# Reordering the projections of a segment-recurrent attention kernel: keys and queries first, a different set of refetched weights, longer scratch runs, small loads on another ring

## Chip, cores, metric

One core of one Trainium2 chip. The metric is device time in microseconds (us) of one execution; lower is better. Kernels that are compared ran on the same chip in alternating rounds.

## The reference, cut to what matters

```python
# A: attention over 64 segments of 32 tokens, with 8 memory rows carried from one to the next
mem = mem0                                             # [1, 8, 1024]
for s in range(64):
    h = concatenate([mem, x[:, 32*s : 32*s + 32]])      # 40 rows of 1024
    q, k, v = h @ Wq, h @ Wk, h @ Wv                    # each 1024 -> 32 heads x 128
    p = softmax(mask(q @ k.T * 128**-0.5))
    o = (p @ v) @ Wo                                    # 32 x 128 -> 1024
    mem = o[:, :8];  outs.append(o[:, 8:])
# B: a gated feed-forward (1024 -> 3584 -> 1024) over the 2048 tokens
return g * a + (1 - g) * b                              # g = sigmoid of a row sum
```

All data are bf16. The four projection matrices are 8 MB each. Cut into pieces of 512 KB that makes 64 pieces, and SBUF has room for 52 of them. So 12 places ("slots") are shared by two pieces, one of each half of the heads, and in every segment 12 pieces are fetched anew.

## The kernel before: the parts concerned

The heads are worked in two halves, `r` = 0 and 1; `ua` and `ub` are the halves that come first and second in this segment (they swap from segment to segment, so what the second half used is still there when the next segment starts). `PAIRS` names the pieces that share a slot. `walk` is the order in which PE (TensorE) goes through the 64 pieces. When a piece has been used and its slot is wanted by another, the fetch of that other is issued at once on SP; SP's weight fetches land in the order of their issue (in all 63 segments of the trace before).

```python
PAIRS = {"k": (0, 2), "q": (0,), "v": (0, 1, 2, 3, 4, 6), "o": (0, 2, 4)}    # 12 shared slots
def seq(m, r):
    ...                                            # p: the paired pieces, f: the others
    return p + f if r == 0 else f + p              # paired ones first in half 0, last in half 1
walk = both(0) + one("v", 0) + both(1) + one("o", 0) + one("v", 1) + one("o", 1)   # both: k, q alternating

def spent(k):                                      # after the piece k has been used
    n = home[k]
    done[n] += 1
    if done[n] < len(uses[n]) and uses[n][done[n]] != k:
        fetch(n)                                   # op("sp", dma_start 512 KB)
```

The hooks of a segment, `on(matrix, half, n, what)` = ahead of the n-th piece of that part. Fills (`f1`, `f2`) are projections of the rows that do not depend on the recurrence, computed some segments early; a fill has eight pieces of PE work.

```python
on("v", 0, 0, lambda: evac(bank_of["k", 0], tok));   on("v", 0, 0, lambda: evac(bank_of["q", 0], tok2))
on("v", 0, 4, lambda: trans(kT, tok));               on("v", 0, 7, lambda: trans(qT, tok2))
on("k", 1, 0, lambda: evac(bank_of["v", 0], vA))     # beside the 16 pieces of the second k and q
on("k", 1, 2, lambda: scores(0))
...
on("o", 0, 0, some(f1, 4)); on("o", 0, 0, lambda: trans(kT, tok)); on("o", 0, 0, some(f1, 2))
on("o", 0, 0, lambda: trans_pe(tok2)); on("o", 0, 0, lambda: attend(ua)); on("o", 0, 0, lambda: attend_tail(ua))
on("o", 0, 0, lambda: trans(qT, None)); on("o", 0, 0, some(f1))
on("o", 0, 1, lambda: scores(1, ...))                # behind the first o piece
on("o", 1, 0, lambda: evac(bank_of["v", 1], vA)); on("o", 1, 0, some(f2, 6))
on("o", 1, 0, lambda: attend(ub)); on("o", 1, 0, lambda: attend_tail(ub)); on("o", 1, 0, some(f2))
```

## Time and profile before

| | before |
|---|---|
| median of 3 runs | 2205.21 us (2203.95 to 2216.17) |
| profiled span, granted TensorE clock | 2213.4 us, 0.988 |
| recurrence | 64 segments, 24.25 us each |
| fetches in a segment | 12 of 512 KB on SP (3 k and q, 6 v, 3 o) |

The strips, the instruction lines and the windows that carry the reading are in the prediction below. Here are two more views. First the page's queues and its chain (the work that ended last, followed back):

```profile
q1 hardware_dynamic: 171760, 466.69, 59.2%
q0 software_dynamic: 30432, 56.99, 8.0%
...
PE 60%; DMA 23%; POOL 6%; DVE 6%; issue 3%; ACT 1%; SPq 0%; DVEq 0%; POOLq 0%
```

q1 is SP's ring with the weights, q0 is POOL's. The chain runs through PE for three fifths of the time and through transfers for a quarter. Then PE's list of waits (who waited for whom: us in total, times, longest us):

```profile
PE pb L690 <- DVE kT L680: 42.6, 29, 12.2
PE pb L796 <- issue: 22.0, 18, 1.9
PE pb L711 <- DVE qT L680: 17.8, 59, 0.3
PE pb L796 <- DMA sl<-in_A_Wk_dram: 13.7, 18, 1.5
PE pb L1025 <- ACT a_bf L677: 13.0, 34, 0.4
```

### The profile page before, as it was taken

The page shows a single profiled execution, that of the slowest core. Times are in us where ns is not written, and L with a number is a line of the kernel's source. Part 1 is how long each engine was busy: PE and PEld are TensorE (multiplying, and loading weights), DVE is VectorE, ACT ScalarE, POOL GpSimd, SP SyncE. Part 2 cuts the span into 40 slices and gives each one's busy share as a digit, 9 for nine tenths or more (in the row PEclk, how much of TensorE's full clock was granted, in tenths as well). Part 3 has the DMA queues.
Part 4 walks back from the last instruction along what each step waited for, and adds up shares of the span by engine and source line. Part 5 has one row for each costly group of instructions (what it writes and reads, how often), then busy time and mean ns, then how long its engine had stood idle before and what let it go on. Part 6 is the DMA issues. An engine that isn't in the chain of part 4 may idle for free.

```text
span 2213.4 us, 76738 instructions
## 1 busy us (share of the span) xinstructions
PE 2034.4 (92%) x37840; PEld 934.4 (42%) x32178; DVE 931.1 (42%) x2154; ACT 606.9 (27%) x1296; POOL 625.2 (28%) x1155
## 2 busy tenths in 40 slices
PE   7789998999999999999989999999888999999999
PEld 4334444444444444444444444444344424343343
DVE  6433343334334434434433344344344516254362
ACT  4322222223222232323322232222222303122130
POOL 7223333432433343243334324333321000000000
PEclk9989999999999999999999999999999999999999
DMA  9978887788888888878887888888789400001000
GB/s 366 389 254 277 297 298 271 270 295 303 281 277 314 297 277 304 310 270 299 304 277 271 287 301 289 275 306 297 274 297 371 150 22 29 30 25 34 20 29 20
DMA packets 202660, 528.84 MB, mean 239 GB/s; under 512 B 29592, under 2 KB 46616, under 8 KB 202336
## 3 DMA queue, kind: packets, MB, share of 16 engines
q1 hardware_dynamic: 171760, 466.69, 59.2%
q0 software_dynamic: 30432, 56.99, 8.0%
q8 instruction: 274, 4.49, 0.8%
q10 hardware_dynamic: 144, 0.26, 0.1%
q14 instruction: 50, 0.41, 0.1%
HBM read 490.16 MB, written 33.55 MB: 237 GB/s over the span
## 4 chain that ended last, share of the span: by engine, by line
PE 60%; DMA 23%; POOL 6%; DVE 6%; issue 3%; ACT 1%; SPq 0%; DVEq 0%; POOLq 0%
PE pb L462 16%; PE pb L796 11%; PE pb L779 8%; PE pb L807 7%; DMA a_scr<-a_bf 7%; DMA sl<-in_A_Wk_dram 6%; PE pb L822 5%; DMA sl<-in_A_Wv_dram 4%; PE pb L1135 4%; PE pb L690 3%; DMA sl<-in_A_Wo_dram 3%; POOL v_scr L863 2%; DVE oT L680 2%; DMA xr_scr<-xr 2%; PE pb L837 1%
## 5 line engine op out<-in xcount | busy, mean ns | idle before, releaser
L796 PE MATMUL pb<-sl,hT 128*32 128x512 bf16 x8192 | 665.0, 381 | 48.6 <-issue 22.0
L779 PE MATMUL pb<-sl,hT 128*32 128x512 bf16 x4096 | 398.0, 379 | 0.0
L796 PEld LDWEIGHTS pb<-sl,hT 128*32 128x32 bf16 x8192 | 210.5, 96 | 429.7 <-issue 274.5
L807 PE MATMUL pb<-sl,oT 128*32 128x256 bf16 x8192 | 282.4, 281 | 19.2 <-issue 11.6
L773 POOL COPY oRc<-oT 128x128 bf16<-128x128 bf16 x128 | 96.1, 750 | 654.3 <-DVE oT L680 648.6
L677 ACT ACTIVATE tok<-pb 128x512 bf16<-128x512 f32 x318 | 176.3, 596 | 346.1 <-PE pb L796 320.6
L807 PEld LDWEIGHTS pb<-sl,oT 128*32 128x32 bf16 x8192 | 206.2, 99 | 83.8 <-ACT oT L677 45.2
L822 PE MATMUL pb<-sl,hR 128*32 128x512 bf16 x3072 | 209.9, 384 | 0.0
L462 PE MATMUL pb<-xT,wg 128*128 128x512 bf16 x768 | 182.8, 381 | 5.0 <-DMA wg<-in_B_w_gate_dram 5.0
L680 DVE COPY kT<-pb 128x512 bf16<-128x512 bf16 x128 | 53.2, 416 | 319.0 <-PE pb L690 287.4
L462 PE MATMUL pb<-xT,wu 128*128 128x512 bf16 x768 | 181.8, 380 | 0.0
L680 DVE CAST oT<-pb 128x256 bf16<-128x256 f32 x256 | 96.7, 419 | 182.9 <-PE pb L762 182.9
L690 PE MATMUL pb<-ident,tok 128*128 128x128 bf16 x1272 | 126.6, 222 | 48.9 <-DVE kT L680 42.6
L1135 PE MATMUL pb<-wd,GT 128*32 128x512 bf16 x1568 | 152.2, 379 | 0.0
L779 PE MATMUL pb<-wd,GT 128*32 128x512 bf16 x1568 | 152.2, 379 | 0.0
L677 ACT ACTIVATE vA<-pb 128x512 bf16<-128x512 f32 x128 | 76.4, 597 | 270.5 <-PE pb L796 270.5
L450 ACT ACTIVATE s<-pb 128x512 f32<-128x512 f32 x112 | 66.9, 597 | 291.5 <-PE pb L462 291.5
L690 PEld LDWEIGHTS pb<-ident,tok 128*128 128x128 bf16 x1272 | 72.0, 98 | 158.8 <-DVE kT L680 90.8
L677 ACT ACTIVATE oT<-pb 128x256 bf16<-128x256 f32 x256 | 84.3, 381 | 189.9 <-PE pb L762 189.9
L451 DVE SCALAR_TENSOR_TENSOR tp<-s,pb 128x512 f32<-128x512 f32 x112 | 76.7, 685 | 125.9 <-ACT s L450 125.5
L726 ACT ACTIVATE E<-pb 128x320 bf16<-128x320 f32 x128 | 56.0, 438 | 220.5 <-DVE pb L725 220.5
L462 PEld LDWEIGHTS pb<-xT,wg 128*128 128x128 bf16 x768 | 75.0, 98 | 97.5 <-issue 8.7
(104 smaller groups left out, 2230.3 us busy)
## 6 DMA issues: line engine op xcount, KB each, us to landing
sl<-in_A_Wv_dram SPq DMA_DIRECT2D x394, 512.0 KB, 9.3
sl<-in_A_Wo_dram SPq DMA_DIRECT2D x205, 512.0 KB, 5.9
sl<-in_A_Wk_dram SPq DMA_DIRECT2D x142, 512.0 KB, 7.3
sl<-in_A_Wq_dram SPq DMA_DIRECT2D x79, 512.0 KB, 6.6
qkr<-qk_scr POOLq DMA_DIRECT2D x126, 64.0 KB, 2.2
qk_scr<-stg POOLq DMA_DIRECT2D x59, 128.0 KB, 6.2
wd<-in_B_w_down_dram SPq DMA_DIRECT2D x7, 1024.0 KB, 14.8
xq_scr<-xTp SPq DMA_DIRECT2D x4, 1024.0 KB, 17.3
```

The lines of the kernel that those rows point to most:

```text
L450: op("act", lambda e: e.activation(s1[:, :], hg, ACTF.Square, scale=SQ), rd=[BK(bg)], wr=[s1.r()])
L451: op("dve", lambda e: e.scalar_tensor_tensor(out=t[:, :], in0=s1[:, :], scalar=1.0, in1=hg, op0=ALU.add, op1=ALU.mult), rd=[BK(bg), s1.r() ...
L462: ins = e.matmul(PB[bk][:, 0:FB], lhsT=w[:, kc, cc:cc + 128], rhs=x[:, :, :, kc, :].rearrange("p t i c -> p (t i) c"), start=(kc == 0), st ...
L677: op("act", lambda e: e.activation(o, i, ACTF.Copy), rd=rd, wr=wr)
L680: op("dve", lambda e: e.tensor_copy(o, i), rd=rd, wr=wr)
L690: ins = e.transpose(to, t[:, j * 128:(j + 1) * 128], ident[:, :])
L773: op("pool", lambda e: e.tensor_copy(oRc[:, u, :, :].rearrange("p c (g j) -> p g j c", g=4), diag), rd=[oT.r()], wr=[oRc.r(128 * u, 128 * ...
L779: return e.add_instruction(mybir.InstMatmult(name=nc.get_next_instruction_name(), start_tensor_calc=start, stop_tensor_calc=stop, tile_siz ...
L796: ins = again(e, g, *at, one, end) if k[0] == "q" else e.matmul(*at, start=one, stop=end)
L807: ins = e.matmul(PB[XO][32 * g:32 * g + 32, 0:256], lhsT=oT[:, gp_, 2 * jj + hh, 0:32], rhs=w[:, c:c + 256], start=(r == 0 and one and hh ...
L822: ins = e.matmul(PB[b][32 * g:32 * g + 32, :], lhsT=h[:, k[2], :], rhs=w[:, g * 512:(g + 1) * 512], start=(n == 0), stop=(n == 7))
L1135: ins = again(e, q, *a, j == 0, j == NJ - 1) if hf else e.matmul(*a, start=(j == 0), stop=(j == NJ - 1))
```

## The change

Intent: with k and q of both halves ahead of most v pieces, softmax of the first half lies beside v work; alternating o and v pieces give the second softmax cover; fills stand where PE waited; copies that ACT did alone are shared by ACT and DVE; scratch rows are stored in longer runs by fewer transfers; small loads leave POOL for SP. The layout of the tiles is shuffled so that vA and qT get other bytes, and one v pair becomes an o pair. The core of the diff (the first and last parts and all of the first segment's special cases are cut):

```diff
-        v_scr = nc.dram_tensor("v_scr", [NSEG, NB, 16, 2, 128], BF16)
+        v_scr = nc.dram_tensor("v_scr", [NSEG, NB, 2, 16, 128], BF16)
...
-        vA = al("vA", [128, 4, 128], at=oT.off)
+        vA = al("vA", [128, 4, 128], at=tok.off)
+        qT = al("qT", [128, 4, 4, 32], at=stage.off)
...
-        PAIRS = {"k": (0, 2), "q": (0,), "v": (0, 1, 2, 3, 4, 6), "o": (0, 2, 4)}
+        PAIRS = {"k": (0, 2), "q": (0,), "v": (0, 1, 2, 3, 4), "o": (0, 1, 2, 3)}
...
-        walk = both(0) + one("v", 0) + both(1) + one("o", 0) + one("v", 1) + one("o", 1)
+        V0 = 3
+        walk = both(0) + one("v", 0)[:V0] + both(1) + one("v", 0)[V0:] + [x for y in zip(one("o", 0), one("v", 1)) for x in y] + one("o", 1)
...
-            op("pool", lambda e: e.dma_start(t[:, :, :].rearrange("p k c -> p (k c)"), xq_scr[s // 4, :, s % 4, :]),
+            op(eng, lambda e: e.dma_start(t[:, :, :].rearrange("p k c -> p (k c)"), xq_scr[s // 4, :, s % 4, :]),   # eng="sp"
...                                            # the same for the loads of qkr and vB; one store of v for four, one of q and k for two
+        def trans8(ka, qa, head=False):        # k and q transposed in one group, two halves of one bank
+            def f(e):
+                trans4(e, ka)
+                return trans4(e, qa, head, 512)
...
+            def turn():
+                heads(kT, "act", 0)
+                heads(qT, "dve", 512)
+            on("k", 1, 1, lambda: trans8(tok, tok2));  on("k", 1, 1, turn)
+            on("k", 1, 3, lambda: scores(ua));         on("k", 1, 3, softmax)
+            on("v", 0, V0, lambda: evac(bank_of["k", 1], tok))
+            on("v", 0, V0, lambda: evac(bank_of["q", 1], tok2))
+            def halves(bank):
+                evac(bank, vA, "act", 0, 256)
+                evac(bank, vA, "dve", 256, 512)
+            on("o", 0, 0, some(fa, 1));  on("o", 0, 0, lambda: trans8(tok, tok2))
+            on("o", 0, 0, lambda: halves(bank_of["v", 0]));  on("o", 0, 0, turn)
+            on("o", 0, 0, some(fa, 2));  on("o", 0, 0, lambda: attend(ua, 0))
+            on("o", 0, 0, lambda: attend_tail(ua, 0))
+            on("o", 0, 0, some(fa, 1));  on("o", 0, 0, lambda: scores(ub));  on("o", 0, 0, softmax)
+            on("o", 0, 0, some(fa, 2))
+            if uw is not None:
+                on("o", 0, 0, lambda: load_oR(Q, uw))
+            on("o", 1, 0, lambda: halves(bank_of["v", 1]));  on("o", 1, 0, some(fa))
+            on("o", 1, 0, lambda: attend(ub, 1));  on("o", 1, 0, lambda: attend_tail(ub, 1))
...
+            on("o", 1, 0, some(fb, 4))
```

## The prediction

> **What bounds the kernel now.** The page of the profiled execution first (2213.4 us; the quoted median is 2205.21), its strips of busy tenths:
>
> ```profile
> PE   7789998999999999999989999999888999999999
> PEld 4334444444444444444444444444344424343343
> ...
> DMA  9978887788888888878887888888789400001000
> ```
>
> Slices 3 to 30 are the recurrence over 64 segments, the rest a dense feed-forward part that the diff leaves alone. In the recurrence both PE and the DMA engines are near full, neither quite. The copies that carry the recurrent rows into the next hT run from 144.5 to 1648.1 us, 63 pairs: (1648.1 - 144.5) / 62 = 24.25 us a segment. Everything depends on that number.
>
> Next the instructions of PE in order of time (start, length, and in brackets the idle time before and who ended it):
>
> ```profile
> 614.18 0.40 PE L690 MATMUL pb<-ident,tok 128*128 128x128 bf16 x4
> ...
> 619.19 0.40 PE L796 MATMUL pb<-sl,hT 128*32 128x512 bf16 x4 [0.96 <-DMA sl<-in_A_Wk_dram]
> ...
> 623.41 0.32 PE L711 MATMUL pb<-mS,ident 128*32 128x320 bf16 x4 [0.30 <-DVE qT L680]
> ```
>
> ```profile
> 651.66 1.47 PE L796 MATMUL pb<-sl,hT 128*32 128x512 bf16 x22 [1.47 <-issue]
> ...
> 657.53 0.40 PE L1025 MATMUL pb<-ident,a_bf 128*128 128x128 bf16 x2 [0.39 <-ACT a_bf L677]
> ...
> 670.73 0.40 PE L690 MATMUL pb<-ident,tok 128*128 128x128 bf16 x4 [0.89 <-DVE kT L680]
> ```
>
> The waits are short, of many kinds, and no kind dominates. Summed between 225 and 1584 us they are 112 us, 2.0 us a segment. Then the same stretch by the DMA engines (columns: window, length, busy of PE, PEld, DVE, ACT, POOL, granted clock, DMA share, GB/s):
>
> ```profile
> 610.60:611.60 1.00, 1.00 (x24) 0.32 (x12) 0.00 (x0) 0.00 (x0) 0.94 (x3) 1.00 0.72 233
> ...
> 613.60:614.60 1.00, 1.00 (x20) 0.43 (x16) 0.35 (x1) 0.00 (x0) 0.00 (x0) 1.00 0.94 202
> ...
> 620.60:621.60 1.00, 1.00 (x18) 0.43 (x15) 0.42 (x1) 0.13 (x1) 0.00 (x0) 1.00 1.07 434
> ...
> 631.60:632.60 1.00, 0.61 (x23) 0.50 (x24) 0.00 (x0) 0.00 (x0) 0.98 (x2) 1.00 0.00 0
> ```
>
> This is one period of the weight stream: 12 fetches of 512 KB that are not resident (two k, one q, six v, three o). For some five us from the segment's start the engines are busy and move 130 to 250 GB/s, then 400 to 430, then for about 3 us nothing, because the next fetch is freed only by the next segment's first piece. At 410 GB/s a fetch is 1.28 us, twelve are 15.4. The landings in the trace (mean of the segments with fills, from the hT copy) say the same: first k 5.4, q 7.7, second k 9.4 to 10.4, then one about every 1.3, last v 18.2, last o 21.8 to 23.1. From the last landing to the end of the segment there are 1.2 to 2.4 us. So PE's chain and the weight stream are tied. Segments 60 and 62, which have no fills and so some 3 us less of PE work, still take 23.2 us.
>
> The stores that fall into the slow stretch, from POOL's order of time, are the third piece:
>
> ```profile
> 659.09 0.55 POOL L1009 DMA_DIRECT2D o_scr<-oRc  x1
> 659.62 2.20 POOL L863 DMA_DIRECT2D v_scr<-stg  x4
> 661.82 0.71 POOL L1035 DMA_DIRECT2D a_scr<-a_bf  x1
> ```
>
> and, from the list of waits,
>
> ```profile
> DVE pA L732 <- DMA a_scr<-a_bf: 34.0, 27, 3.1
> ```
>
> POOL issues six to ten transfers one after another around each boundary, 0.55 us each, and the store of a_bf comes last although pA (same bytes) waits for it.
>
> **What the Trainium skill says.** "DMA: Bandwidth & Descriptors", section "Why small descriptors are slow (HBM only)", gives each packet a fixed overhead, 27% for 256 bytes; its table "Specifications" asks for 512 B or more. The change turns 256 B runs of the k/q and v stores into 512 B and 1 KB. The trace agrees in sign only: weight packets of 4 KB took about 160 ns at mid-segment and about 250 ns in the slow stretch; it does not say which store did it. The same page, section "Issuing engines are not separate DMA queues", says that a transfer moved from POOL to SP saves only issue time: here 0.55 us of POOL for some 0.4 us of SP. "Perfetto Trace Analysis", section "Identifying the Most-Contended Engine", warns that matmul busy time overstates how near PE is to its limit; agreed, as the four concurrent matmuls of a piece are each shown as 379 ns while a piece starts every 0.216.
>
> **The change part by part, per segment.** First PE. From the listing, 16 k/q pieces take 3.46 us (0.216 each), seven o pieces 1.53 (0.22). Work that stays: 48 x 0.216 = 10.4; 16 x 0.22 = 3.5; fills, 12 pieces on average x 0.216 = 2.6; Wo fills 4 x 0.21 = 0.8. Sum 17.3. Scores 2 x 0.31, attend with tail and its bubbles 2 x 0.45, the end of the segment (last product, copy, transpose, copy) 0.5: 2.0.
> - Transposes: four groups and on average one of a fill, each 0.42 (0.10 of drain before, three starts of 0.056, 0.15 after): 2.1 now. Merged into groups of eight (0.10 + 7 x 0.056 + 0.15 = 0.64), two and on average half a one: 1.6. Saves 0.5.
> - Waits, 2.0 in idle time and 0.85 as bubbles that count as busy (24.25 - 17.3 - 2.0 - 2.1 = 2.85). The softmax of the first half now begins before the rest of v and is 3.8 us long (616.1 to 619.9) against some 4.5 us of PE work up to its use, so the kT wait of 0.9 goes. qT gets its own bytes: the 0.30 goes. The second softmax lies beside 16 alternating o and v pieces (3.5 us) and fills. The a_bf wait (0.39) is covered by four fill pieces (0.86). New small waits, worked from the copy times of the groups table (ACT 128x512 0.60, DVE 0.42, halves 0.38 and 0.42): tok2 before the second group of eight 0.15; vA before attend 0.2 in each half; kT by ACT behind half of vA 0.1 in each half. Sum 0.75.
> - PE after: 17.3 + 2.0 + 1.6 + 0.75 = 21.7.
>
> Then the stream. Still 12 fetches, one v less and one o more (2 KB packets at 84 ns against 4 KB at 159, so 0.07 us more). Five small loads leave POOL and are issued on SP about 3 us earlier; v stores are one issue instead of four, q and k share one; the a_bf store is among the first. I choose that this takes 1.3 us out of the slow stretch; the trace cannot give it. Second k then lands at 8.1 to 9.1 and is needed at 8.3 to 9 (piece 34 of 64 plus scores and transposes, five v pieces earlier than now): a wait of 0.3 on average. v0 to v2 follow, v3 and v4 by 14.8; the o fetches are freed at 13.3 to 14.6 and land at 16.9 to 21.0. After the last o piece come now 0.86 us of fill and 0.5 of end: 21.0 + 0.2 + 1.4 = 22.6.
>
> Stream 22.6, PE 21.7 + 0.3 for the second k = 22.0. I take 22.5, since the stream's end binds in most segments. Saving 24.25 - 22.5 = 1.75 a segment, 63 segments: 110 us. Prologue and feed-forward unchanged to within a few us. 2205 - 110 = 2095.
>
> **The rivals.**
> - The stream decides alone and longer runs do nothing. Then the last o lands at 22.3, the fills after it add 0.86 with the DMA engines idle, the segment stays at 24: within 2%, 2185 to 2200. For it: segments without fills barely faster. Against: in two segments of four the last landing lies 2.4 us before the end, so PE's own waits bind there.
> - The second k becomes the wait: its window shrinks by about a microsecond, from 8.3 to 7.3 (some 36 pieces to 31), and 0.96 is already lost at 619. If the slow stretch stays, 1.5 to 2 us go back there and the gain is 0.5 a segment, 2170.
> - The stream's slow stretch vanishes almost wholly (it costs 2.6 to 3.6 us against 1.28 a fetch). Then PE binds at 21.5: 2205 - 173 = 2032.
> - SP's ring is in order: a small load whose data or buffer is late holds back the weight fetches behind it. Against: all three are freed before the segment's end, data written segments ago. If it happens, 0.5 us a segment, 30 us lost.
>
> **Range and chances.** The low end is the third rival with some waits left, 2035; the high end lies between the first two, 2165. Above 2161 the change is within 2%: the first rival or a strong second one, together 0.12; slower by 2% needs a stall that I don't see, 0.03; faster 0.85.
>
> **What would show it.** Period of the hT copies 22 to 23; the waits for kT, qT and a_bf gone; PE's idle time near 1 us a segment; DMA share above 0.88 with fewer windows below 250 GB/s near the boundary; the a_bf store landing before pA asks for it; waits left on Wk or Wo. Wrong if Wk waits exceed 1 us a segment, if the slow stretch is as long as now, or if the period stays above 23.5.

## More of the kernel before

Every operation is recorded through one helper, which works out the waits from what is read and written. For PSUM it goes by the bank: engines that touch one bank wait for one another.

```python
if kind == "P":                                    # a PSUM bank
    b = self.banks.setdefault(reg[1], {})
    deps.extend(o for eng, o in b.items() if eng != op.eng)
    b[op.eng] = op
```

## The result, and the profile after

The changed kernel takes **2371.12 us** (median of 4, 2364.87 to 2380.57), the kernel before in the same rounds 2209.35 us: ratio 1.073, 95% interval 1.068 to 1.079. It is slower by 7%. A ratio is the mean time of one kernel's fast runs over that of the other's of the same rounds, so it is not quite the ratio of the medians quoted. The profiled span is 2373.7 us at a clock of 0.958.

The page of the changed kernel (strips as before; PEclk is the granted clock in tenths):

```profile
PE   7778888888888888888888888888787999999999
...
PEclk9989999989999999999999999999988999999999
...
DMA  9967777777877877778878887777878910001000
...
q1 hardware_dynamic: 216240, 483.68, 59.8%
q0 software_dynamic: 22400, 40.56, 5.2%
...
PE 58%; DMA 34%; DVE 3%; ACT 2%; issue 1%; POOL 1%; SPq 1%; POOLq 0%; DVEq 0%; ACTq 0%
```

In the recurrence PE is at 8 where it had been at 9, and the DMA engines, which should have become fuller, went from 8 to 7. Both are less busy: this suggests that something is now in series that was in parallel. The chain names transfers for 34% in place of 23%, and the o weights alone for 16% in place of 3%. PE's list of waits:

```profile
PE pb L812 <- DMA sl<-in_A_Wo_dram: 100.4, 105, 3.6
PE pb L755 <- DVE vA L680: 62.1, 126, 1.0
PE pb L850 <- DMA oR<-o_scr: 42.2, 23, 3.2
PE pb L801 <- DVE hT L680: 18.2, 59, 0.3
PE pb L801 <- DMA sl<-in_A_Wk_dram: 11.5, 19, 1.8
```

PE's waits for kT and a_bf are gone, as intended, and so is DVE's wait for pA (34.0 us before, none after); qT's fell to 10.6 us. In their place stand o weights, vA, and the rows of o for the fills. One segment shows all of it. PE, in order of time (start, length, idle before it and its releaser in brackets):

```profile
702.91 0.30 PE L755 MATMUL pb<-tA,vA 32*128 32x64 bf16 x16 [0.39 <-DVE vA L680]
...
705.43 0.39 PE L812 MATMUL pb<-sl,oT 128*32 128x256 bf16 x8
...
710.02 0.29 PE L755 MATMUL pb<-tA,vA 32*128 32x64 bf16 x16 [0.52 <-DVE vA L680]
...
711.25 1.69 PE L812 MATMUL pb<-sl,oT 128*32 128x256 bf16 x48
714.06 0.40 PE L812 MATMUL pb<-sl,oT 128*32 128x256 bf16 x8 [1.12 <-DMA sl<-in_A_Wo_dram]
715.34 0.40 PE L812 MATMUL pb<-sl,oT 128*32 128x256 bf16 x8 [0.87 <-DMA sl<-in_A_Wo_dram]
```

The first o piece of the segment, at 705.43, frees the first o slot. Its successor and three others are needed from 712 on, and the last two come 1.12 and 0.87 us late. The second vA of this segment, ACT first and then DVE:

```profile
709.13 0.38 ACT L677 ACTIVATE vA<-pb 128x256 bf16<-128x256 f32 x1 [3.58 <-PE pb L801]
```

```profile
709.54 0.42 DVE L680 CAST vA<-pb 128x256 bf16<-128x256 f32 x1 [1.72 <-ACT vA L677]
```

DVE had been idle for 1.72 us and starts 0.03 us after ACT's half has ended: the two halves come out of one bank, and they run one after the other. They take 0.83 us together; the single ACT copy of the kernel before takes 0.597 and lay beside other work. Last, the weight stream and the clock in the same segment (columns as in the prediction's windows):

```profile
703.00:704.00 1.00, 1.00 (x52) 0.74 (x51) 0.96 (x3) 0.62 (x2) 0.00 (x0) 1.00 1.02 389
...
705.00:706.00 1.00, 0.80 (x24) 0.57 (x28) 0.50 (x2) 0.44 (x1) 0.95 (x2) 1.00 0.49 176
706.00:707.00 1.00, 1.00 (x40) 0.77 (x32) 0.90 (x4) 0.00 (x0) 0.00 (x0) 1.00 0.62 139
707.00:708.00 1.00, 1.00 (x36) 0.70 (x28) 0.79 (x3) 0.00 (x0) 0.00 (x0) 1.00 0.80 119
708.00:709.00 1.00, 1.00 (x32) 0.74 (x28) 0.00 (x0) 0.00 (x0) 0.00 (x0) 1.00 0.97 373
...
717.00:718.00 1.00, 0.73 (x8) 0.28 (x8) 0.19 (x1) 0.47 (x2) 0.94 (x3) 0.50 0.00 0
```

For three microseconds in the middle of the segment the stream falls to 119 to 176 GB/s: the v fetches are running out when the first o fetch is issued at 705.87, and that fetch's first packet starts only at 707.05. On average over the segments the DMA engines are busy 0.63, 0.69 and 0.83 of the three microseconds from 14 us after the first k issue; in the kernel before it was 1.00, 0.89 and 0.96. And after the late o pieces the clock is at 0.50, from 716.2 to 719.6 us. In the whole run the records show the clock at half for 202 us, before for 55. The Trainium skill describes such a fall in "TensorE: Matmul & The Clock Gate", section "HAM oscillation — how this bites in real kernels": a wait for data that crosses a window of some 3.4 us lets PE fall back to half rate, and the loss is half of the time at that rate. The trace agrees in the length (31 of the 44 stretches last 3.41 us, 10 more twice that), but not in the waits: here they were 1.12 and 0.87 us. As to the loss, from 717.27 to 718.95 PE's k and q pieces start every 0.42 us, and every 0.22 in the same segment at full clock.

The landings say it most clearly. From the trace, mean of 50 segments, us from the issue of the segment's first k fetch:

```
                         k     q     k   | v ...                                     | o ...
before   landed        4.66  7.02  8.96 | 10.74 12.26 13.57 14.86 16.15 17.47      | 18.85 20.40 21.83
         o issued                                                                    13.70 14.74 15.16
after    landed        4.89  7.10  8.50 | 10.64 12.00 13.47 14.97 16.27            | 18.60 20.64 22.32 23.91
         o issued                                                                    14.27 14.71 15.50 16.20
```

Once several fetches are queued, one lands every 1.3 to 1.6 us. Before, the ring (SP's queue of fetches) holds v fetches until 17.5 us and the o fetches, issued 2.3 to 3.8 us ahead of that, follow at 1.4 to 1.6 us. After, the first o is issued only 2.0 us ahead of the last v's landing at 16.27; it needs 4.3 us from issue to landing and comes 2.33 us behind the last v, and the next comes 2.04 behind it. The last o lands 2.1 us later than before, and the segment is longer by 2.4.

### The profile page after: what moved, and what is told of

Its sections match the earlier page's. It is cut to its first block, busy times and chain, and to the rows that moved or that the text cites. A ratio compares the mean times of both kernels' runs of the same rounds, so it can differ in the third digit from the quotient of the medians.

```text
span 2373.7 us, 77419 instructions
## 1 busy us (share of the span) xinstructions
PE 2059.2 (87%) x38220; PEld 970.0 (41%) x32556; DVE 1007.0 (42%) x2249; ACT 607.0 (26%) x1330; POOL 429.6 (18%) x776
## 4 chain that ended last, share of the span: by engine, by line
PE 58%; DMA 34%; DVE 3%; ACT 2%; issue 1%; POOL 1%; SPq 1%; POOLq 0%; DVEq 0%; ACTq 0%
DMA sl<-in_A_Wo_dram 16%; PE pb L463 15%; PE pb L801 13%; PE pb L784 9%; DMA sl<-in_A_Wk_dram 8%; PE pb L812 5%; PE pb L831 4%; DMA oR<-o_scr 4%; PE pb L1160 4%; DMA sl<-in_A_Wv_dram 3%; PE pb L691 3%; PE pb L850 2%; PE pb L1138 1%; DVE vA L680 1%; ACT vA L677 1%
## 5 line engine op out<-in xcount | busy, mean ns | idle before, releaser
L801 PE MATMUL pb<-sl,hT 128*32 128x512 bf16 x8192 | 742.2, 389 | 34.3 <-DVE hT L680 18.2
L812 PE MATMUL pb<-sl,oT 128*32 128x256 bf16 x8192 | 368.0, 286 | 107.1 <-DMA sl<-in_A_Wo_dram 100.4
L784 PE MATMUL pb<-sl,hT 128*32 128x512 bf16 x4096 | 415.0, 395 | 0.0
L801 PEld LDWEIGHTS pb<-sl,hT 128*32 128x32 bf16 x8192 | 225.3, 98 | 369.3 <-issue 217.8
L831 PE MATMUL pb<-sl,hR 128*32 128x512 bf16 x3072 | 248.4, 403 | 21.9 <-DMA sl<-in_A_Wv_dram 10.7
L677 ACT ACTIVATE tok<-pb 128x512 bf16<-128x512 f32 x253 | 144.1, 596 | 221.6 <-PE pb L801 216.8
L680 DVE CAST a_bf<-pb 128x128 bf16<-128x128 f32 x64 | 18.7, 292 | 342.8 <-ACT a_bf L677 342.8
L680 DVE CAST tok<-pb 128x512 bf16<-128x512 f32 x93 | 64.0, 689 | 170.8 <-PE pb L784 170.8
L850 PE MATMUL pb<-sl,oR 128*32 128x256 bf16 x2016 | 78.4, 304 | 44.4 <-DMA oR<-o_scr 42.2
L463 PEld LDWEIGHTS pb<-xT,wu 128*128 128x128 bf16 x768 | 75.1, 98 | 90.9 <-DMA wu<-in_B_w_up_dram 0.4
L455 DVE SCALAR_TENSOR_TENSOR tp<-tp,pb 128x512 f32<-128x512 f32 x112 | 77.0, 687 | 77.9 <-ACT tp L454 77.9
## 6 DMA issues: line engine op xcount, KB each, us to landing
wd<-in_B_w_down_dram SPq DMA_DIRECT2D x7, 1024.0 KB, 14.9
```

Of the source, the lines that this page charges most:

```text
L455: op("dve", lambda e: e.scalar_tensor_tensor(out=t[:, :], in0=t[:, :], scalar=1.0, in1=hu, op0=ALU.add, op1=ALU.mult), rd=[BK(bu), t.r()], ...
L463: ins = e.matmul(PB[bk][:, 0:FB], lhsT=w[:, kc, cc:cc + 128], rhs=x[:, :, :, kc, :].rearrange("p t i c -> p (t i) c"), start=(kc == 0), st ...
L677: op("act", lambda e: e.activation(o, i, ACTF.Copy), rd=rd, wr=wr)
L680: op("dve", lambda e: e.tensor_copy(o, i), rd=rd, wr=wr)
L784: return e.add_instruction(mybir.InstMatmult(name=nc.get_next_instruction_name(), start_tensor_calc=start, stop_tensor_calc=stop, tile_siz ...
L801: ins = again(e, g, *at, one, end) if k[0] == "q" else e.matmul(*at, start=one, stop=end)
```

## The experiments

In the table, a period of the recurrence and PE's idle time in it are split by who ended the wait (us a segment, 61 segments, matmul records of the trace). "PE" is the period less its idle time, and includes the loss by the half clock.

| kernel | median us | ratio to before | period | PE | idle | Wo | Wk, Wq, Wv | vA | oR | other | half clock | last o lands |
|---|---|---|---|---|---|---|---|---|---|---|---|---|
| before | 2209 | 1 | 24.27 | 22.18 | 2.08 | 0.04 | 0.32 | 0.05 | 0 | 1.67 | 0.45 | 21.83 |
| after | 2371 | 1.073 | 26.66 | 22.52 | 4.13 | 1.58 | 0.30 | 0.95 | 0.64 | 0.66 | 2.63 | 23.91 |
| e4_no_o | 2148 | 0.973 | 23.19 | 21.14 | 2.05 | 0 | 0.51 | 0.95 | 0 | 0.59 | 0.06 | none |
| f2_bno_o | 2192 | 0.992 | 23.94 | 22.07 | 1.88 | 0 | 0.24 | 0.05 | 0 | 1.59 | 0.34 | none |
| f1_bpairs | 2293 | 1.037 | 25.42 | 22.79 | 2.63 | 1.32 | 0.07 | 0.05 | 0 | 1.19 | 1.45 | 23.65 |
| e8_v6p | 2282 | 1.032 | 25.46 | 21.87 | 3.59 | 0.60 | 0.71 | 0.96 | 0.14 | 1.18 | 0.90 | 22.97 |
| g5_order | 2239 | 1.014 | 24.62 | 21.91 | 2.71 | 0.15 | 1.49 | 0.08 | 0 | 0.99 | 0.34 | 22.01 |

The first theory was: PE's own chain did get shorter, as the prediction had it, and what is lost is lost to the o fetches. The rival: the new order of PE is slower in itself, by the copies that were not parallel.

### e4_no_o and f2_bno_o: the o weights are never fetched anew

Wrong: a shared o slot keeps the piece of one half for both (the result still passes within its tolerance).

```diff
-            if done[n] < len(uses[n]) and uses[n][done[n]] != k:
+            if done[n] < len(uses[n]) and uses[n][done[n]] != k and k[0] != "o":
```

e4 is the changed kernel with this line, f2 the kernel before with it.

> The changed kernel, but the o weights are never fetched again once they lie in their slots (wrong result on purpose): 8 fetches a segment instead of 12, everything else the same. Theory W (the o fetches are freed too late and the last one's landing sets the segment's end): PE's waits for Wo (some 180 us over PE and its weight loads) go to nothing, the period falls from 26.6 to about 23.5, time near 2180, ratio 0.99. Rival S (the small loads on SP's ring, the vA and oR waits and the lower granted clock carry the loss): at most 86 us of idle time go, time 2285 or more, ratio above 1.03.

> The kernel before, with the o weights never fetched again (wrong on purpose), the twin of e4_no_o. It shows what PE's own chain costs before the change. If the weight stream was nearly the bound before (as the prediction has it, tied), the time falls a little: period 23 to 23.5, 2130 to 2160, ratio 0.97. If the stream was not on the path before, ratio 0.99 to 1. If the new order is a better chain on PE, as intended, e4_no_o (0.9725) is below this one.

Measured: 2148.47 us (ratio 0.973, 0.969 to 0.976) and 2191.94 (0.992, 0.990 to 0.994). Without o fetches the changed order is faster than the order before by 43 us. So the o stream costs the changed kernel 2371 - 2148 = 223 us and cost the kernel before 18. That settles the first question: PE's chain is better, the stream takes it all back and more. Per segment after and e4 differ by 3.47 us. The table accounts for 3.3 of them: Wo 1.58, oR 0.64, and half of (2.63 - 0.06) of half clock, 1.29 (an estimate), together 3.5, less the 0.2 by which the other weight waits are shorter in after. What stays in e4 is the 0.95 for vA.

```profile
PE pb L755 <- DVE vA L680: 62.5, 127, 1.0
PE pb L801 <- DMA sl<-in_A_Wk_dram: 25.8, 37, 2.3
PE pb L801 <- DVE hT L680: 18.5, 59, 0.3
```

(PE's waits in e4.) f2 missed its first forecast (2130 to 2160): by the fork written ahead of it, the o fetches were not on the path before. Without them a segment takes 23.94 us, with them 24.27, and PE's wait for Wo was 0.04. So PE's chain, with the k and v fetches that it needs, bound, and the stream's end lay behind it without setting the time; f1, next, shows how little room there was.

### f1_bpairs and e1_pairs: the shared pieces alone, both ways

f1 puts a fourth o pair in the place of the sixth v pair in the kernel before, e1 takes it back in the changed kernel (its second line only puts the copies of oT in the order in which the o pieces then use them).

```diff
 f1 (on before)
-        PAIRS = {..., "v": (0, 1, 2, 3, 4, 6), "o": (0, 2, 4)}
+        PAIRS = {..., "v": (0, 1, 2, 3, 4), "o": (0, 2, 4, 6)}
 e1 (on after)
-        PAIRS = {..., "v": (0, 1, 2, 3, 4), "o": (0, 1, 2, 3)}
+        PAIRS = {..., "v": (0, 1, 2, 3, 4, 5), "o": (0, 1, 2)}
-            for g in range(4) if r == 0 else (2, 3, 0, 1):
+            for g in range(4) if r == 0 else (1, 2, 3, 0):
```

> The kernel before with five v pairs and four o pairs, the one part of the change that moves a fetch to the end of the stream. Theory W: the last landing moves about 1.3 us later in the half of the segments where it binds; 64 x 0.7 to 1.3 = 45 to 85 us, ratio 1.02 to 1.04. If the pairs do not matter by themselves, ratio 1.00.

> The changed kernel with six v pairs and three o pairs again, as before the change (12 fetches all the same). Theory W: one o fetch of 1.3 us less lies between the last release and the end; 64 x 1.3 = 83 us, time near 2290, ratio 1.035. Rival S: no change, 2350 to 2390, ratio 1.065 to 1.08.

Measured: f1 2293.39 us (1.037, 1.031 to 1.043), e1 2339.01 (1.060, 1.056 to 1.064). One line on the kernel before, with the same twelve fetches of the same size, costs 84 us, as much as half of the whole loss. In f1 the last v lands at 16.1 us in place of 17.5, the first o at 17.9 and the last at 23.65. PE's first wait in its list:

```profile
PE pb L807 <- DMA sl<-in_A_Wo_dram: 83.4, 84, 2.8
```

A v slot is free at 3.5 to 6.3 us, so its fetch keeps the ring full. An o slot is free at 13.7 or later, when the ring is about to run empty, and its piece is needed some 8 us later. Moving one fetch from the first kind to the second lengthens exactly the part of the stream that has no slack. Taking it back in the changed kernel gives only 32 us, because there the last v slots are free late as well (with V0 = 3 the last two v fetches of the changed kernel go out at 9.8 and 10.2 us, before at 5.8 and 6.3): Wv becomes a wait, 1.63 us a segment with Wk and Wq, where Wo falls to 0.68.

### e8_v6p: e1 with six v pieces ahead of the second k

```diff
-        V0 = 3
+        V0 = 6
```

> The changed kernel with six v and three o pairs and with six v pieces (V0 = 6) ahead of k and q of the second half, so that all six v fetches are freed in one burst near the segment's start and the ring is never empty before the o fetches come, as before the change. Theory W with the drained ring as its second part: the last o lands about 2 us earlier than in the changed kernel, Wo and Wv waits mostly go, and so do the stretches of half clock that follow them; time 2230 to 2270, ratio 1.01 to 1.03. If the order of v does not matter, as e1_pairs: ratio 1.06.

Measured: 2282.22 us (1.032, 1.027 to 1.036), 57 us better than e1. Now v fetches go out from 3.9 to 6.8 us and the ring is full until 17.3. Still the o fetches, issued at 14.9 to 16.1, land at 19.5 to 22.97, as PE reaches its first o piece 1.2 us later than before. Pairs and V0 together explain 89 of the 162 us.

### e2_pool, e5_noalt, e3_oR: three parts that were suspected

Each is the changed kernel with one part undone: e2 puts the small loads (qkr, hT, vB) back on POOL; e5 runs all o pieces of the first half ahead of the second v; e3 loads the o rows for the fills several pieces earlier.

```diff
 e2
-        def load_h(s, eng="sp"):
+        def load_h(s, eng="pool"):          # qkr and vB likewise
 e5
-        walk = ... + [x for y in zip(one("o", 0), one("v", 1)) for x in y] + one("o", 1)
+        walk = ... + one("o", 0) + one("v", 1) + one("o", 1)
 e3
-                on("o", 0, 0, lambda: load_oR(Q, uw))
+                on("v", 0, V0, lambda: load_oR(Q, uw))
```

> The changed kernel with the loads of qkr, hT and vB issued by POOL again. Theory W: these loads stand behind the o fetches in SP's ring and nothing on the path waits for them, so the time stays within 1% of the changed kernel, ratio 1.06 to 1.085. Rival S (they slow or hold up the weight stream): the time falls by 50 us or more, ratio below 1.05.

> The changed kernel with all o pieces of the first half ahead of all v pieces of the second, as before the change. Theory W: the last o pair is freed 3 v pieces (0.65 us) earlier, so the Wo waits shrink by about that: 64 x 0.65 = 40 us, time near 2330, ratio 1.055. If alternation is what hides the second softmax, the time rises instead.

> The changed kernel with the load of oR issued after the third v piece instead of after the attention of the first half. PE waits 42 us for it now. Theory W: that wait lies ahead of the Wo wait in the same segments, so taking it away only lengthens the Wo wait; within 15 us of the changed kernel, ratio 1.065 to 1.08. If the waits add up, 42 us go, ratio 1.055.

Measured: 2376.9, 2376.3 and 2372.68 us, all within 0.3% of the changed kernel. e2: the ring of the small loads does not matter, as the prediction took from the skill. e5: the o fetches are issued at 14.29, 14.71, 15.58 and 16.25 us, no earlier than with alternation, because SP needs 0.4 to 0.9 us from one issue to the next. e3: the wait for oR (0.64 a segment) is gone, and Wo grew from 1.58 to 2.05; half clock and vA stay. A wait that lies ahead of a later wait is worth little while the later one stands.

### g1_own: are the copies in series because of the bank?

e4 with vA copied by one ACT instruction, and q transposed into a bank of its own.

```diff
             def halves(bank):
-                evac(bank, vA, "act", 0, 256)
-                evac(bank, vA, "dve", 256, 512)
+                evac(bank, vA, "act")
...
-            on("o", 0, 0, lambda: trans8(tok, tok2))
-            on("o", 0, 0, turn)
+            on("o", 0, 0, lambda: trans8(tok, tok2, qb=F2))    # B1 at the first turn
+            on("o", 0, 0, lambda: turn(F2))
```

> The changed kernel without the refetching of o weights (as e4_no_o, 2148 us, 23.2 us a segment; the o arithmetic is wrong on purpose), and in it two more edits: vA is copied by one ACT instruction in place of an ACT half and a DVE half, and q is transposed into a PSUM bank of its own in place of the other half of kT's bank. Theory 'one bank, one engine at a time': in the changed kernel the pairs of copies that were to run side by side follow one another, because they read one bank. Then the single copy gives back 0.384 + 0.424 - 0.591 = 0.22 us twice a segment, and qT (0.425 us) no longer starts after kT (0.594 us), which takes away the 0.34 us that scores wait, twice: 0.8 to 1.1 us a segment, 63 segments, 2080 to 2100 us. Rival 'the next wait takes its place' (softmax, or the last of the fetches): above 2130 us.

Measured: 2127.06 us (0.963, 0.959 to 0.966). The waits fall as the theory says: vA from 0.95 to 0.34 a segment (and 0.13 in gaps too short to be put down to anyone), qT from 0.17 to none. But the time falls by 21 us and not by 50 to 70, as the waits for Wk and Wv grow from 0.51 to 0.84. The time lies between the two forecasts: the bank is the cause of the series, and part of what it costs is then taken by the waits for k and v pieces. The copies of kT and qT show the cause in one line each. In the changed kernel (first fence), with both in one bank, qT starts 0.03 us after kT has ended; in g1 (second fence), with two banks, both start at once:

```profile
696.37 0.60 ACT L677 ACTIVATE kT<-pb 128x512 bf16<-128x512 bf16 x1 [1.24 <-PE pb L691]
697.00 0.42 DVE L680 COPY qT<-pb 128x512 bf16<-128x512 bf16 x1 [1.56 <-ACT kT L677]
```

```profile
658.67 0.60 ACT L677 ACTIVATE kT<-pb 128x512 bf16<-128x512 bf16 x1 [1.24 <-PE pb L691]
658.67 0.42 DVE L680 COPY qT<-pb 128x512 bf16<-128x512 bf16 x1 [0.94 <-PE pb L691]
```

Two halves of vA in two banks were not tried. The rule behind it is in the Trainium skill, "PSUM — Partial Sum Buffer", section "PSUM bank collisions raise a hardware error": two engines must not be in one bank and partition quadrant at once. The kernel's helper keeps this by the bank, so two engines that read halves of one bank are never side by side. (No run here broke the rule.)

### g2_late, g4_late6, g3_all, g5_order: releasing the o slots earlier

g2 is the changed kernel with three fill pieces moved from ahead of the first o piece to behind the second v, and four from behind the second attend to ahead of it. g4 has the same on e8. g3 adds to g4 the two edits of g1 and the early oR load of e3. g5 then spreads the fills again, with the first o pieces in one block (the walk of e5, with V0 = 6).

```diff
 g2
             on("o", 0, 0, lambda: attend_tail(ua, 0))
-            on("o", 0, 0, some(fa, 1))
             on("o", 0, 0, lambda: scores(ub))
             on("o", 0, 0, softmax)
-            on("o", 0, 0, some(fa, 2))
...
             on("o", 1, 0, some(fa))
+            on("o", 1, 0, some(fb, 4))
             on("o", 1, 0, lambda: attend(ub, 1))
             on("o", 1, 0, lambda: attend_tail(ub, 1))
...
-            on("o", 1, 0, some(fb, 4))
 g5 (on g3)
-            on("o", 0, 0, some(fa, 1))
+            on("o", 0, 0, some(fa, 2))
...
-            on("o", 1, 0, some(fa))
-            on("o", 1, 0, some(fb, 4))
+            on("v", 1, 0, some(fa))
+            on("o", 1, 0, some(fb, 3))
             on("o", 1, 0, lambda: attend(ub, 1))
             on("o", 1, 0, lambda: attend_tail(ub, 1))
+            on("o", 1, 0, some(fb, 3))
```

> The changed kernel with all fetches and pairs as they are; only PE's order differs: the three fill pieces between the first attend and the first o0 piece move behind the v1 and o0 pieces, and four fill pieces go ahead of the second attend instead of behind it. A fill piece is about 0.4 us of PE. Theory 'window': the o fetches are released 1.2 us earlier, their use is not earlier, and the fills also cover the copy of the second vA; the last o lands near 22.7 us after the first k issue in place of 23.9, the waits for Wo (180 us with PE's loads) fall to a third or less, and the kernel is at 2260 to 2310 us. Rival 'rate': the fetches land late because the stream moves them slowly whatever their issue; then last landing stays at 23.5 to 24 and the time within 1.5% of 2371. Rival 'copy only': the gain is only the covered vA, 0.55 us a segment, some 2335 us.

> The order of g2_late on the kernel of e8_v6p (2282 us: six v and three o pairs, all but two of the v0 pieces ahead of the second k). Theory 'window': its o fetches, issued at 14.9 to 16.1 us, come 1.2 us earlier; the period falls from 25.5 to about 24.3 us and the time to 2200 to 2235 us, level with the kernel before. Rival 'rate': it stays above 2255 us.

> g4_late6 with the two edits of g1_own (vA by one ACT copy, q transposed into its own bank) and the o rows for the fill loaded earlier. This is the attempt at a version that beats both. If the bank waits are on the path here as well: another 0.5 to 0.9 us a segment, 2150 to 2195 us, faster than before by up to 2.5%. If the stream decides by now (twelve fetches of which the last lands at 22 us or later), it stays with g4_late6 within 1%.

> g3_all (2256 us; 3.25 us of PE idle a segment, of which v pieces waiting for Wv 0.88, oT behind the second attend 0.54, the transposes for the tokens 0.34) with only fill pieces moved and o0 as one block ahead of v1: two fills ahead of the transposes, the rest of the first eight between o0 and v1, three of the second eight ahead of the second attend, three behind it. If these waits are covered and no other takes their place: period 24.9 to 23.2-23.7 us, 2150 to 2185 us. If the o stream (last landing about 22 us) keeps the end: 24.2 to 24.5, 2200 to 2225 us. If waits only change their place: above 2235 us.

Measured: 2372.25, 2323.46, 2255.87 and 2239.48 us (1.076, 1.053, 1.021, 1.014). g2 brought nothing, and g4 is 41 us slower than e8. The o fetches did come earlier (first issue 13.8 in g2 against 14.27, last landing 23.57 against 23.91; in g4 22.03 against 22.97) and the Wo wait fell to 0.95 and 0.06. In g2 it was 0.4 us earlier and not the 1.2 expected: 0.4 us is the length of one fill matmul, while fill pieces start every 0.22 us, so three of them are 0.65. And my edit had made two new waits: four of the moved fill pieces read oR, whose load had stayed where it was, and the o copies behind the second attend had nothing beside them any more. From PE's waits in g2:

```profile
PE pb L850 <- DMA oR<-o_scr: 87.8, 30, 5.3
PE pb L812 <- DMA sl<-in_A_Wo_dram: 61.4, 68, 2.5
PE pb L812 <- ACT oT L677: 31.4, 64, 0.5
```

So g2 and g4 tell less than they were made for. g3 and g5, without these, do: Wo is at 0.05 and 0.15 us a segment, the half clock at 0.28 and 0.34, and the loss of 162 us has shrunk to 45 and 32; neither brought the gain hoped for (g5 came out as the last case of its forecast, waits that only change their place). What is left in g5 is at the other end of the stream (PE's waits in g5):

```profile
PE pb L831 <- DMA sl<-in_A_Wv_dram: 50.3, 73, 1.2
PE pb L801 <- DMA sl<-in_A_Wk_dram: 32.5, 42, 2.3
```

Its last o lands at 22.01 us, before it was 21.83. The stream has not become faster in any of these kernels, and a PE that arrives earlier waits for it.

### h1_keep, h3_keepb, h2_keep5: is a stream that starts from an empty ring slow?

In every kernel so far the first fetch of a segment lands 4.7 to 5.3 us after its issue and the next 2.2 to 2.5 us later. One o piece is fetched once more (the same bytes into the same slot), ahead of the first k fetch (by 1.8 us on average in h3, 2.0 in h2, 5.5 in h1); h1 is on e4, h3 on the kernel before, h2 on g5.

```diff
+            def again_o(k=("o", ub, PAIRS["o"][0])):
+                t = slots[home[k]]
+                op("sp", lambda e: e.dma_start(dst(t, k), src(k)), wr=[t.r()], lane=f"sl{home[k]}")
+            if not last:
+                on("o", 1, 6, again_o)
```

> e4_no_o (no o refetched; eight fetches a segment, the stream idle for 7 us before each segment) with one weight fetch more per segment, 512 KB, put in some 2.5 us ahead of the segment's first k fetch. Theory 'empty queue': any first fetch after a pause takes 4.5 to 5 us, and the added one takes this upon itself; then the first k lands 3.0 to 3.8 us after its issue in place of 5.06, the second k at 5.5 to 6.8 in place of 8.83, in spite of the 512 KB more. Rival 'segment start': the start is slow because of what else runs then; the fetch ahead makes it later, first k at 5.0 or more, second k at 9 to 10. Time: 2110 to 2140 us under the first (e4_no_o 2148, of which 0.41 us a segment waits for Wk), 2150 to 2180 under the second.

> The kernel before with the same extra fetch (an o piece fetched once more into its own slot, with the same data, so results stay right), behind its three o fetches. Here the last o lands about 2.4 us before the first k issue, so the pause is short. Theory 'empty queue': first k lands at 3.2 to 4 us in place of 4.66, second k at 6.5 to 7.5 in place of 8.96, and the waits for kT's tokens and Wk (0.6 us a segment) shrink: 2170 to 2205 us. Rival 'segment start': everything 1.3 us later, 2230 to 2300 us.

> g5_order with the extra fetch of h3_keepb. Theory 'empty queue': the stream of each segment ends 1 to 1.5 us earlier, 20 to 50 us below g5_order. Rival 'segment start': 20 to 80 us above it, for 512 KB more per segment that the stream has to move.

Measured: 2389.23, 2258.34 and 2278.24 us. h1 cannot be used for its time: the fills at the segment's end read that slot and waited 162 us for the fetch, which I had overlooked; its extra fetch, with only small loads beside it, landed 4.9 us after its issue (median 4.3). h2 is 39 us above g5. h3 costs 50 us and is clear: the second k lands at 9.87 us in place of 8.96, and the extra fetch itself was moved at the usual pace. Packet times from h3's trace (mean ns of a packet of the weights that starts in that microsecond, from the first k issue):

```
us       -1..0        0..1   1..2   2..3   3..4   4..5   5..6   6..7   7..8   8..9
ns       266 (few)      91     98    235    226    261    253    171    161    162
KB each   2              2   2       4      4      4      4      4      4      4
```

The 2 KB packets up to 2 us are the extra fetch, close to the 88 ns they take elsewhere. Then come the first k and the first q with 4 KB packets of 226 to 261 ns, where the fetches behind them have 161. In the microsecond from 1 to 2 POOL's ring moves some 175 KB beside them, and the packets of the extra fetch are as quick as elsewhere. "Empty ring" is out as the cause of the slow packets. It is not out as a delay: the extra fetch too landed 4.4 us after its issue, about as late as the first o fetch of the changed kernel (4.3).

### h4_krows and g6_best: rows, place in SBUF

h4 is the kernel before with other pieces of k and q in the three shared slots.

```diff
-        PAIRS = {"k": (0, 2), "q": (0,), ...
+        PAIRS = {"k": (2, 4), "q": (2,), ...
```

> The kernel before with other k and q pieces as the ones that are fetched anew: pieces 2 and 4 of k and 2 of q in place of 0 and 2 of k and 0 of q; same sizes, same slots, same times. Theory 'rows': pieces 0 of Wk and Wq are slow to read; then all three fetches run at 160 to 175 ns a packet, the third lands at about 7.2 us after the first issue in place of 8.96, and the waits for kT's tokens and Wk (0.65 us a segment) mostly go: 2165 to 2195 us. Rival 'place': the first two are slow again (240 ns or more), third landing at 8.6 to 9.2 us, time within 1% of before.

Measured: 2213.58 us, ratio 1.000 (0.995 to 1.006). Packets of 275 and 239 ns for the first two fetches, 162 for the third: it is not the rows.

g6 is g5 with V0 = 7, the second q copied by DVE, the second set of fills between o and v, and the two shared k slots in another part of SBUF. (The q slot was meant to move too. But slots are numbered matrix by matrix, so slots 0 to 2 are k's two and a resident k piece, and q's is slot 14: built, g6 has k's slots at bytes 28288 and 32384 in place of 2048 and 6144, and q's at 73344 as in g5.)

```diff
-        V0 = 6
+        V0 = 7
-        slots = [... at=RING + n * PIECE if n < NLOW else None ...]
+        slots = [... at=RING + (n - 3) * PIECE if 3 <= n < 3 + NLOW else None ...]
-            on("v", 0, V0, lambda: evac(bank_of["q", 1], tok2))
+            on("v", 0, V0, lambda: evac(bank_of["q", 1], tok2, "dve"))
-            on("v", 1, 0, some(fa));  on("o", 1, 0, some(fb, 3))
+            on("v", 1, 0, some(fb, 4));  on("o", 1, 0, some(fa))
```

> g5_order (2239 us, 24.6 us a segment, 2.7 us of it PE idle) with four edits. Seven of eight v0 pieces ahead of the second k (its Wk wait, 0.53 us a segment, comes later and should halve); the copies of the second k and q side by side on ACT and DVE, from two banks; between o0 and v1 four pieces of the second set of fills in place of the rest of the first set, whose v pieces waited there for Wv (0.79 us a segment); and the three slots that k and q are fetched into exchanged with three others in another part of SBUF. If the covered waits are gains: 23.3 to 23.9 us a segment, 2150 to 2195 us, and the first kernel here that beats the one before. If the o stream (last landing 22 us after the first k issue, as in g5_order) keeps the end: 24.2 us or more, 2205 to 2235 us. Of the slots: if the place in SBUF made the first two fetches slow, their packets fall from 230-280 ns to 160-175 and the third lands near 7.5 us; if not, they stay.

Measured: 2258.24 us (1.022, 1.019 to 1.026): no gain, and slower than g5 (1.014, 1.010 to 1.017). The slow packets stayed (258, 230, then 168 ns), so for k it is not the place in SBUF; for q this stays untested. The weight waits at the two places did halve or vanish, and the copy that I gave to DVE, which is in the first softmax at that time, became a wait of its own: in all 64 segments it starts right behind softmax's last instruction on DVE (PE's waits in g6):

```profile
PE pb L691 <- DVE tok L680: 79.4, 60, 2.1
```

No version here beats the kernel before with right results.

## Why the prediction was wrong, point by point

**Which views bound it, right in part.** It called PE's chain and the stream tied. f2 (23.94 without o fetches, 24.27 with) says that PE's chain bound and the end of the stream cost 0.33 us; f1 says that the stream came close behind, as one fetch moved to its end cost 84 us. In the change one chain got shorter, the other longer, and the longer one is the time.

**PE after, 21.7 (22.0 with the second k): too low by 1.2.** e4 measures 23.19. The work without waits was well predicted (20.95, measured 21.14). The waits were not: 0.75 + 0.3 predicted, 2.05 measured. The term "vA before attend 0.2 in each half" is 0.95 in sum; the prediction took the two halves of the copy as parallel, and they are in series by the bank. It also did not see that in the new order the last v piece of the first half stands three fill pieces and a group of transposes ahead of its attend, where it had 16 pieces and more in between. The wait for the second k was 0.41 in e4 against 0.3. Waits named as going did go: kT and a_bf; qT fell from 17.8 us to 10.6.

**The stream after, 22.6: too low by 4.1; this is the step that failed.** The o fetches are released 2.3 us later than predicted, take 1.3 us more from the last release to the last landing, and 0.4 us more lies between that and the end of the segment. The prediction's clock starts at the hT copy, some 0.7 us ahead of the first k issue (its landings of the kernel before against those above: 5.4 and 4.66, 18.2 and 17.47). In its own words, in four places:
- "I choose that this takes 1.3 us out of the slow stretch": the second k lands 0.46 us earlier (8.50 against 8.96). The longer runs, the fewer stores and the other ring together gave no more than that (the ring alone nothing, by e2). And the slow packets are not due to them: in the changed kernel 4 KB packets take 246 and 251 ns in microseconds (2 to 4) in which POOL's ring moves 4 to 5 KB.
- "v3 and v4 by 14.8": the last v lands at 17.0 in that clock. The five v fetches take 7.8 us from the second k's landing, where five at 1.28 would take 6.4; with V0 = 3 the last two of them are issued only at 9.8 and 10.2.
- "The o fetches are freed at 13.3 to 14.6": they are issued at 15.0 to 16.9 in that clock. The fills, the second scores and the waits now stand ahead of the first o piece.
- "and land at 16.9 to 21.0": 19.3 to 24.6. The prediction has 6.4 us from the last release to the last landing, and it took 7.7, as the v fetches were running out when the first o was issued. The diff's fourth o pair was booked as "0.07 us more"; f1 measures it at 84 us on the kernel before, where nothing else was changed. There it is the largest part found by a single edit; in the changed kernel, where the late v slots stand beside it, taking it back gives 32 us, and V0 then 57.

**A term that was missing: the clock.** Late o weights let PE idle at the end of each segment, and the records show 2.63 us a segment at half clock against 0.45, that is an estimated 1.1 us more of PE time, if the loss is half of it. The prediction had no rival in which waits cost more than their length.

**The rivals.** "The stream decides alone" was the right mechanism, sized at 24 us a segment with the last o at 22.3. The second k as a wait, and the ring in order, did not come. Of the prediction's signs of failure, the period above 23.5 came, and nearly so the slow stretch as long as now.

**What stays open.** Why the first two fetches of a segment have packets of 216 to 278 ns. Not an empty ring (h3), not the rows (h4), not the place of k's slots (g6; q's did not move), not which ring the small loads use (e2). One rival was left untested: in every run the two are a piece of Wk and the piece of Wq with the same number, and they are never fetched apart. And the share of each order effect, as they do not add up (the pairs are 84 us alone, 32 here): undone one after the other, the shared pieces and V0 give 89 of 162 us (e8), and the releases, oR, the banks and the order of the fills 43 more (g5). Of the last 32 the table shows only that PE waits for weights 1.3 us a segment more in g5 than before; which part of the change is behind that was not tested.

## What to carry to other kernels

When weights are refetched in a loop, the moment at which a slot becomes free counts as much as the bytes: choose for sharing the pieces whose slot is free early and needed late, and follow each release to its landing before moving work ahead of it. Splitting a PSUM copy over two engines gained nothing here while both halves lay in one bank (0.83 us against 0.60). And ask of a wait that you remove which wait stands behind it: here e3, g1, g2 and g4 all removed waits, and the time fell by less than their length or not at all.

## What the Trainium skill lacked or had wrong

- "DMA: Bandwidth & Descriptors": no section has a slow start of a burst of fetches. Here 4 KB packets of the first two fetches of each segment take 216 to 278 ns and most of those behind them 160 to 190, counted by fetch in all the kernels, and the cause was not found.
- The same page, section "Latency and other measured facts", gives some 600 ns to the first byte for SP's transfers. Here the first packet of a fetch on an empty ring starts 1.0 us after the start of the issuing instruction (itself 0.34 us long), which fits; but a segment's first fetch of 512 KB needed 4.7 to 5.3 us to land, and the page has a sum for POOL's path alone (section "Anatomy of one DMA — SWDGE (gpsimd) path": about 2.0 us and the bytes at 436 GB/s, an estimate of 3.2 us).
- No page gives the spacing of issues on SP as a measured time; the nearest is a count of sequencer cycles in that page's part on trn3 B0. Here it is 0.4 to 0.9 us between two fetches of 512 KB, so four slots that become free together are released over 1.9 us.
- "TensorE: Matmul & The Clock Gate", section "HAM oscillation — how this bites in real kernels", advises against idle gaps of over some 3.4 us (the section behind it says that PE can also oscillate from short idles, without a length). Here half clock followed windows with two gaps of 1.12 and 0.87 us, in which PE was busy for 41% of the time; over the 44 times that it happened, the longest gap in the 4.5 us before had a median of 1.2 us, and was under 3 us in 43 cases.
